# A linear-attention and MLP block on one core: projections in 64-row array tiles, key-value sums over blocks of both signs, and a token-major query side

## The chip, the core and the metric

The kernel runs on one core of a Trainium2 chip. The core has a matrix engine (PE, with its weight loads listed apart as PEld), a vector engine (DVE), a scalar engine (ACT), a general engine (POOL), a sequencer that here only issues DMAs (SP), and 16 DMA engines that all queues share. The metric is the device time of one execution in microseconds (us); lower is better. The kernel before takes 407.46 us, the median of three runs from 407.23 to 407.73.

## The reference

```
x: 1 x 2048 x 576 (bf16), 32 heads of 18;  LN = layer norm over the last axis
qkv   = LN(x) @ wqkv                          # 576 -> 3 x 576
pq,pk = q @ w_phi[h], k @ w_phi[h]            # per head, 18 -> 18
phi_q = [softmax(pq), softmax(-pq)]           # per head, 18 + 18 features
phi_k = [softmax(pk), softmax(-pk)]
kv    = sum_s phi_k[s]^T v[s];  z = sum_s phi_k[s]
o     = (phi_q @ kv) / (phi_q . z + 1e-6)
h     = x + o @ wo
h2    = h + gelu(LN(LN(h)) @ w1 + b1) @ w2 + b2   # 576 -> 4608 -> 576
```

The softmax over 18 features needs no maximum here: both kernels exponentiate and divide by the sum.

## The kernel before

The 2048 tokens are 16 token tiles of 128. `w_phi` is folded into the key and query weights first: the weight is transposed (`flip`, or five DMA transposes in `turn_wq`) and multiplied by a block-diagonal matrix of `w_phi` (`fold`, L271), so that one product gives all of pk or pq.

**Front: projections.** Each token tile is normalised on DVE (`normalise`, L208; some tiles on ACT, L236) and turned to feature-major form: the first four tiles on PE (`transpose_to`, L249), the others by DMA transposes (L243). The 576 features are cut into five chunks of 128 rows, the last one half empty. `project` (L307) multiplies one token tile by the value weights (`pv`) or the folded key weights (`pk`): five chunks by two column halves of 288, ten matmuls. ACT copies the values out (L318) and exponentiates the keys twice, with plus and minus sign (L329). DVE sums each head's features and inverts (`total`, L334), and POOL multiplies the keys by that (`weigh`, L342; L346). Queries are made the other way round (`ask`, L287): the folded weights are the stationary operand and 512 tokens the moving one, so the exponentials `eT` come out feature-major; 20 such units of five matmuls are spread between the key and value tiles. Query softmax sums are not taken at this point.

**Sums.** When all keys are weighed, `sums` (L505) makes ten accumulations over the 16 token tiles, one for each of five head groups and each of the two signs (`pkv`, L510; 160 matmuls), and DVE masks them to the block diagonal in `kvm` (L519, L524). `kvm` holds 20 columns a head: 18 values, the normaliser, and a column of ones that yields the query's softmax sum.

**Combine.** `combine` (L531) multiplies a token tile's `eT` by `kvm` in ten matmuls, in two units of heads (`pn`, L543). The two signs are weighted crosswise with each other's softmax sum: ACT copies those sums out (L551, L552), DVE multiplies (L555), POOL adds the signs (L561), DVE inverts and divides (L564, L565). The result `ob` is turned: on PE for tiles 0 to 3 (L586), by DMA for the rest (L582). `residual` (L591) multiplies by `wo` (ten matmuls `pa`, L598), adds to x and takes statistics on DVE; `rescale` writes the doubly normalised tile twice, side by side, into `ln2`; `turn2` (L619) turns it.

**MLP.** Eight strips of 256 tokens. `up` (L729) has 18 pairs of F-tiles; each pair is 9 chunks of 64 features by two matmuls that use rows 0-63 and rows 64-127 of the array (`ph`, L737), and ACT applies GELU (L761). `down` (L767) is 144 matmuls per strip (`po`, L782), then DVE adds (L786) and SP stores (L787). Between them `mlp` (L798) places the residual of the next strip's two tiles and the combines of the strip after that at given positions of `down` (`marks`).

**What sets the order.** PE and POOL follow the program text throughout. ACT, DVE and SP follow it through the front, up to `front.close()`; afterwards a scheduler orders them. A queue runs in order and stands still while its first instruction waits. All loads, stores and DMA transposes but three go through SP's queue. `w1` is loaded in two parts of six DMAs of 432 KB (`load_w1`, L417): the first at tile 11, the second, followed by twelve DMAs of `w2` (L720), once the keys' and values' memory is free, which is after the last of the sums.

```
nc.tensor.matmul(ph[half][:, cols], w1[..][rows, c, ..], x[rows, c, cols], ..)   # up, rows = 64 of 128
for m in range(0, NM // 2, 3): ... nc.sync.dma_start(w2[:, m0:m0+3, :], ..)      # L718-720, after load_w1(1)
work_ = [enter(a), enter(a+1), combine(b,0), leave(b), combine(b+1,0), leave(b+1)]; marks = [2,24,46,66,86,106]
```

Of the kernel before, what the change touches and what calls it, by code (L numbers as in the profile page):

```python
# [8 lines left out]
P = 128  # L9
# [11 lines left out]
NC = 5  # L21
# [7 lines left out]
NW = DH + 2  # L29
TB = 256  # L30
UNITS = [(0, 3), (3, 5)]
UH = 21
KC = 9
KH = 64


@with_exitstack
def kernel(
# [16 lines left out]
    NB = S // 512  # L55
    NS = S // TB
    TPS = TB // P

# [6 lines left out]
    e_pool = ctx.enter_context(tc.tile_pool(name="e_pool", bufs=4))  # L65
# [4 lines left out]
        tc.manual_schedule(engines={mybir.EngineType.PE, mybir.EngineType.Pool})  # L70
    )
    front = ctx.enter_context(ExitStack())
    front.enter_context(
        tc.manual_schedule(
            engines={
                mybir.EngineType.Activation, mybir.EngineType.DVE, mybir.EngineType.SP,
# [5 lines left out]
    wqp = persist.tile([P, NC, DP], BF16, name="wqp", tag="wqp")  # L82
    wo = persist.tile([P, NC, D], BF16, name="wo", tag="wo")
    kvm = persist.tile([P, NG, 2, 7 * NW], BF16, name="kvm", tag="kvm")
# [6 lines left out]
    ob = [persist.tile([P, DP], BF16, name=f"ob{i}", tag=f"ob{i}") for i in range(2)]  # L91

    psA = ctx.enter_context(ExitStack())
    two = psA.enter_context(tc.tile_pool(name="two", bufs=3, space=bass.MemoryType.PSUM))
    one = psA.enter_context(tc.tile_pool(name="one", bufs=2, space=bass.MemoryType.PSUM))
    w1_pool = ctx.enter_context(tc.tile_pool(name="w1_pool", bufs=1, side="left"))
    kctx = ctx.enter_context(ExitStack())
    kpool = kctx.enter_context(tc.tile_pool(name="kpool", bufs=1, side="left"))
    inner = ctx.enter_context(ExitStack())
    wpool = inner.enter_context(tc.tile_pool(name="wpool", bufs=1, side="right"))  # L100

    phik = [kpool.tile([P, 2, D], BF16, name=f"phik{t}", tag=f"phik{t}") for t in range(NT)]
    vals = kpool.tile([P, NT, NH, VW], BF16, name="vals", tag="vals")
    w1 = [w1_pool.tile([P, KC, FF // 4], BF16, name="w1_0", tag="w1_0")]
    wv = wpool.tile([P, NC, D], BF16, name="wv", tag="wv")
    wT = wpool.tile([P, NG, DP], BF16, name="wT", tag="wT")
    wkp = wpool.tile([P, NC, D], BF16, name="wkp", tag="wkp")
    bd = wpool.tile([P, NG, 7, DH], BF16, name="bd", tag="bd")
    wph = wpool.tile([P, NG, DH], BF16, name="wph", tag="wph")
    lnb = [wpool.tile([P, DP], BF16, name=f"lnb{i}", tag=f"lnb{i}") for i in range(6)]  # L110
# [8 lines left out]
    def scratch(n):  # L119
        e = e_pool.tile([P, NG, 2, 512], BF16, name="eT", tag="eT")  # L120
        flat = e[:, :, :, :].rearrange("p g s t -> p (g s t)")[:, 0 : NC * n]
        return flat.rearrange("p (c f) -> p c f", c=NC)

    wk = scratch(D)
    wq = scratch(DP)
    wphi_rows = A_w_phi.rearrange("h d f -> (h d) f")
    nc.scalar.dma_start(xh[:, 0:1, :], x_v[:, 0:1, :])
# [5 lines left out]
    nc.sync.dma_start(xh[:, 1:2, :], x_v[:, 1:2, :])  # L133
    load_rows(wv, A_wqkv[:, 2 * D : 3 * D])
    nc.sync.dma_start(xh[:, 2:4, :], x_v[:, 2:4, :])
    nc.sync.dma_start(xh[:, 4:8, :], x_v[:, 4:8, :])
    for c in range(NC):
        m = P if c < NC - 1 else 64
        src = A_wqkv[c * P : c * P + m, 0 : NG * 126]
        nc.sync.dma_start(  # L140
            wq[:m, c, :].rearrange("p (g f) -> p g f", g=NG)[:, :, 0:126],
            src.rearrange("p (g f) -> p g f", g=NG),
        )
    nc.sync.dma_start(xh[:, 8:16, :], x_v[:, 8:16, :])
# [15 lines left out]
    nc.gpsimd.memset(kvm[:, :, :, :], 0.0)  # L160
    for t_ in (wk, wv):
        nc.vector.memset(t_[64:P, 4, :], 0.0)
    nc.vector.memset(wq[64:P, 4, :], 0.0)
    nc.vector.memset(wq[:, :, :].rearrange("p c (g f) -> p (c g) f", f=P)[:, :, 126:P], 0.0)
    for i in range(6):
        nc.vector.memset(lnb[i][:, D:DP], 0.0)
    nc.vector.memset(wkp[64:P, 4, :], 0.0)
    spare = small.tile([P, 4], FP32, name="spare", tag="spare")
    nc.scalar.copy(spare[:, :], mhalf[:, :])
    nc.scalar.activation(  # L170
        vals[:, :, :, DH],
        ident[:, 0:NH].rearrange("p (o h) -> p o h", o=1).to_broadcast([P, NT, NH]),
        AF.Identity, bias=ones7[:, 0:1], scale=0.0,
    )
# [9 lines left out]

    def warm(n):
        pw = two.tile([P, P], BF16, name="pw", tag="two")
        for _ in range(n):
            nc.tensor.transpose(pw[:, :], ident[:, :], ident[:, :])

    def inverse(mv, n, bias, scale, eng=nc.vector):  # L190
        va = small.tile([P, 2], FP32, name="va", tag="va")
        eng.tensor_scalar(va[:, 0:n], mv[:, 0:n, 1], scale, bias, ALU.mult, ALU.add)  # L192
        rs = small.tile([P, 2], FP32, name="rs", tag="rs")
        nc.gpsimd.tensor_tensor(rs[:, 0:n], va[:, 0:n], mhalf[:, 0:n], ALU.pow)  # L194
        return rs

    def statistics(tiles, bias, scale, eng):
        n = len(tiles)
        mv = small.tile([P, 2, 2], FP32, name="mv", tag="mv")
        for i, t in enumerate(tiles):  # L200
            st = small.tile([P, 2, nc.vector.BN_STATS_DIM], FP32, name="st", tag="st")
            nc.vector.bn_stats(st[:, 0, :], xh[:, t, 0:HALF])
            nc.vector.bn_stats(st[:, 1, :], xh[:, t, HALF:D])
            nc.vector.bn_aggr(mv[:, i, :], st[:, :, :])
        return mv, inverse(mv, n, bias, scale, eng)
# [5 lines left out]

    lnT = [lnt_pool.tile([P, NC, 512], BF16, name="lnT", tag="lnT") for _ in range(NT // 4)]
    moments, shifts = {}, {}
# [8 lines left out]
    def measure(*tiles):  # L222
        mv, rs = statistics(tiles, EPS, 1.0, nc.vector if tiles[0] < 4 else nc.gpsimd)
        for i, t in enumerate(tiles):
            moments[t] = (mv, rs, i)
            if t >= 8 and t % 2:
                shifts[t] = shift(mv, rs, i)

    def turned(t):
        b, j = divmod(t, 4)  # L230
        return lnT[b][:, :, j * P : (j + 1) * P]

    def scale(t):
        if t >= 8 and t % 2:
            mv, rs, i = moments[t]
            nc.scalar.activation(  # L236
                lnb[t % 6][:, 0:D], xh[:, t, :], AF.Identity,
                bias=shifts[t][:, :], scale=rs[:, i : i + 1],
            )
        else:  # L240
            normalise(lnb[t % 6][:, 0:D], xh[:, t, :], *moments[t])
        if t >= 4:
            nc.sync.dma_start_transpose(turned(t), lnb[t % 6][:, :])  # L243

    def turn_wq(c0, c1):
        for c in range(c0, c1):
            nc.sync.dma_start_transpose(wT[:, :, c * P : (c + 1) * P], wq[:, c, :])

    def transpose_to(src, dst, copy=nc.scalar.copy):  # L249
        pT = one.tile([P, DP], BF16, name="pT", tag="one")  # L250
        for c in range(NC):
            nc.tensor.transpose(
                pT[:, c * P : (c + 1) * P], src[:, c * P : (c + 1) * P], ident[:, :]
            )
        copy(dst, pT[:, :].rearrange("p (c q) -> p c q", c=NC))  # L255
# [14 lines left out]

    def fold(wp, c, copy):  # L271
# [10 lines left out]
        copy(wp[:m, c, 0:D].rearrange("p (i f) -> p i f", i=2), pW[:m, :, 0:HALF])  # L282

    eT = {}
    banks = {"q": (one, "one")}

    def ask(b, g):  # L287
        if g == 0:
            eT[b] = e_pool.tile([P, NG, 2, 512], BF16, name="eT", tag="eT")
        pool, tag = banks["q"]  # L290
        pq = pool.tile([P, 512], FP32, name="pq", tag=tag)

        def part(c0, c1):
            for c in range(c0, c1):
                nc.tensor.matmul(  # L295
                    pq[:, :], wqp[:, c, g * 126 : g * 126 + P], lnT[b][:, c, :],
                    start=(c == 0), stop=(c == NC - 1),
                )

        part(0, 2)  # L300
        yield
        part(2, NC)
        yield
        nc.scalar.activation(eT[b][:, g, 0, :], pq[:, :], AF.Exp, scale=1.0)
        nc.scalar.activation(eT[b][:, g, 1, :], pq[:, :], AF.Exp, scale=-1.0)

    def project(dst, lhs, w):  # L307
        for c in range(NC):
            for i in range(2):
                nc.tensor.matmul(  # L310
                    dst[:, i, 0:HALF], lhs[:, c, :], w[:, c, i * HALF : (i + 1) * HALF],
                    start=(c == 0), stop=(c == NC - 1),
                )

    def value(t):
        pv = two.tile([P, 2, 512], FP32, name="pv", tag="two")
        project(pv, turned(t), wv)
        nc.scalar.copy(  # L318
            vals[:, t, :, 0:DH].rearrange("p (i h) d -> p i h d", i=2),
            pv[:, :, 0:HALF].rearrange("p i (h d) -> p i h d", d=DH),  # L320
        )

    rk = {}

    def key(t):
        pk = two.tile([P, 2, 512], FP32, name="pk", tag="two")
        project(pk, turned(t), wkp)
        for s in range(2):
            nc.scalar.activation(  # L329
                phik[t][:, s, :].rearrange("p (i f) -> p i f", i=2),  # L330
                pk[:, :, 0:HALF], AF.Exp, scale=1.0 - 2.0 * s,
            )
# [94 lines left out]
    def more():  # L427
        for _ in ask(*next(asked)):
            pass
# [427 lines left out]
```

## Time and profile before

| | value |
|---|---|
| median of three runs | 407.46 us (407.23 to 407.73) |
| span of the profiled execution | 405.5 us |
| span against that median | 2.0 us less |
| PE busy | 398.6 us, 98% |
| ACT, DVE, POOL busy | 196.8, 175.8, 107.0 us |
| up, first pair starts | 90.16 us |
| first matmul of the first down | 111.85 us |
| a strip of the MLP, steady state | 39.12 us (133.23 to 172.35) |

The profile was taken by the hardware on one execution; its own time is the span of 405.5 us, from the first to the last instruction, and the runs' median lies 2.0 us above it. A group's line reads: line of the program, engine, operation, tile written and tiles read, shapes, count; busy time of the group and mean time of one; idle time of the engine before it. Matmuls overlap, so the mean of one matmul is longer than its share of the engine: 324 matmuls of `up` take 17.79 us in the chain, 54.9 ns each, though one lasts 269 ns. Where this text gives a pace, it is such a quotient. The row "to landing" is the time from a DMA's issue to the arrival of its completion.

### The profile page before, as it was taken

The numbers are of one execution on the slowest core, as the hardware profiler recorded it, in microseconds if no ns is written. First come the engines' busy times: TensorE is split into PE (matmuls) and PEld (weight loads), VectorE is DVE, ScalarE is ACT, GpSimd is POOL, SyncE is SP. The second block draws the span as 40 slices with busy tenths as digits, with TensorE's granted clock in tenths as the row PEclk, the third lists the DMA queues.
The fourth block names the chain that finished last, engine by engine and source line by source line (L and its number), as shares of the span: only waits on it lengthen the run. The fifth ranks groups of instructions, "written<-read, shape, count | busy, mean of one in ns | idle before, by whom it ended". The sixth has DMA issues, their size and how long they took to land.

```text
span 405.5 us, 11185 instructions
## 1 busy us (share of the span) xinstructions
PE 398.6 (98%) x4882; PEld 324.2 (80%) x4882; DVE 175.8 (43%) x393; ACT 196.8 (49%) x468; POOL 107.0 (26%) x146
## 2 busy tenths in 40 slices
PE   7999999999999999999999999999999999999996
PEld 7786667758888888788888888888888888778875
DVE  5899975683466007601750274037204620510000
ACT  6888985388710680077008502840283048206800
POOL 5479994221214102310240023003200410111010
PEclk9999999999999999999999999999999999999999
DMA  8973586099712102200320032003200310220000
GB/s 250 229 109 49 129 169 131 17 224 325 229 32 61 32 2 53 49 23 2 60 51 15 2 70 52 2 3 73 49 3 14 78 33 3 19 55 18 2 16 15
DMA packets 52011, 27.83 MB, mean 69 GB/s; under 512 B 40506, under 2 KB 49274, under 8 KB 51834
## 3 DMA queue, kind: packets, MB, share of 16 engines
q1 hardware_dynamic: 51216, 26.95, 29.3%
q8 instruction: 38, 0.62, 0.6%
q10 hardware_dynamic: 746, 0.17, 0.2%
q14 instruction: 11, 0.09, 0.1%
HBM read 15.87 MB, written 2.36 MB: 45 GB/s over the span
## 4 chain that ended last, share of the span: by engine, by line
PE 90%; DMA 5%; DVE 1%; ACT 1%; SPq 1%; issue 1%; POOL 0%; DVEq 0%; ACTq 0%
PE ph L737 35%; PE po L782 35%; PE pa L598 5%; PE pv L310 3%; PE pq L295 3%; PE pk L310 3%; DMA w<-in_B_w_dram 2%; PE pn L543 2%; PE pkv L510 2%; DMA wT<-eT 1%; DMA eT<-in_A_wqkv_dram 1%; PE pW L276 1%; SPq L421 1%; DVE ln L208 0%; PE pT L586 0%
## 5 line engine op out<-in xcount | busy, mean ns | idle before, releaser
L761 ACT ACTIVATE h<-ph,b1col 128x256 bf16<-128x256 f32 x288 | 120.5, 470 | 75.0 <-PE ph L737 56.3
L782 PE MATMUL po<-w,h 128*128 128x288 bf16 x1152 | 148.7, 286 | 0.0
L737 PE MATMUL ph<-ln2T,w 64*128 64x256 bf16 (+1 forms) x2646 | 143.8, 267 | 0.0
L737 PEld LDWEIGHTS <-w 64*128 64x128 bf16 x2646 | 125.8, 94 | 17.1 <-issue 2.1
L782 PEld LDWEIGHTS <-h 128*128 128x128 bf16 x1152 | 110.9, 98 | 28.3 <-issue 1.5
L602 DVE TENSOR_TENSOR xh<-pa,xh 128x288 bf16<-128x288 f32 x32 | 14.4, 450 | 112.3 <-PE pa L598 112.3
L194 POOL TENSOR_TENSOR rs<-va,mhalf 128x1 f32<-128x1 f32 (+1 forms) x26 | 15.2, 583 | 155.3 <-DVE va L192 154.8
L551 ACT COPY sw<-pn 128x21 f32<-128x21 f32 (+1 forms) x32 | 5.6, 174 | 97.4 <-PE pn L543 97.3
L561 POOL TENSOR_TENSOR uu<-tt 128x399 f32<-128x399 f32 (+1 forms) x32 | 26.6, 832 | 69.7 <-DVE tt L555 67.8
L310 PEld LDWEIGHTS <-lnT 128*128 128x128 bf16 x320 | 30.7, 98 | 9.7 <-ACT lnT L255 0.3
L786 DVE TENSOR_TENSOR ot<-po,hb 128x288 bf16<-128x288 f32 x32 | 14.5, 453 | 53.9 <-PE po L782 53.9
L346 POOL TENSOR_TENSOR phik<-phik,rk 128x576 bf16<-128x576 bf16 x30 | 35.1, 1195 | 3.4 <-DVE rk L340 3.4
L772 POOL TENSOR_TENSOR hb<-xh,b2bc 128x576 f32<-128x576 bf16 x16 | 20.4, 1273 | 54.5 <-DVE ot L786 51.6
L555 DVE TENSOR_TENSOR tt<-pn,sw 128x798 f32<-128x798 f32 (+1 forms) x32 | 25.1, 785 | 6.9 <-ACT sw L552 6.8
L295 PE MATMUL pq<-lnT,wqp 128*128 128x512 bf16 x100 | 24.9, 379 | 0.1
L598 PE MATMUL pa<-wo,oT 128*128 128x288 bf16 x160 | 22.2, 286 | 0.1
L310 PE MATMUL pv<-wv,lnT 128*128 128x288 bf16 x160 | 22.2, 286 | 0.0
L310 PE MATMUL pk<-wkp,lnT 128*128 128x288 bf16 x160 | 22.1, 286 | 0.1
L336 DVE TENSOR_REDUCE sk<-phik 128x64 f32<-128x1152 bf16 x16 | 21.2, 1323 | 1.9 <-ACT phik L329 1.8
L565 DVE TENSOR_TENSOR ob<-uu,rec 128x378 bf16<-128x378 f32 (+1 forms) x32 | 21.0, 656 | 1.1
L329 ACT ACTIVATE phik<-pk 128x576 bf16<-128x576 f32 x32 | 19.2, 656 | 3.6 <-PE pk L310 3.6
L208 DVE TENSOR_SCALAR ln<-xh,mv,rs 128x576 bf16<-128x576 bf16 x31 | 16.3, 567 | 7.3 <-POOL rs L194 7.3
(82 smaller groups left out, 245.3 us busy)
## 6 DMA issues: line engine op xcount, KB each, us to landing
w<-in_B_w_dram SPq DMA_DIRECT2D x24, 432.0 KB, 9.1
out_dram<-ot SPq DMA_DIRECT2D x16, 144.0 KB, 1.8
xh<-in_A_x_dram SPq DMA_DIRECT2D x1, 1152.0 KB, 7.0
eT<-in_A_wqkv_dram SPq DMA_DIRECT2D x4, 157.5 KB, 6.3
eT<-in_A_wqkv_dram SPq DMA_DIRECT2D x1, 576.0 KB, 5.0
wv<-in_A_wqkv_dram SPq DMA_DIRECT2D x1, 576.0 KB, 6.5
xh<-in_A_x_dram SPq DMA_DIRECT2D x1, 576.0 KB, 7.6
wo<-in_A_wo_dram SPq DMA_DIRECT2D x1, 576.0 KB, 4.2
```

What stands on the lines that cost most here:

```text
L295: nc.tensor.matmul(pq[:, :], wqp[:, c, g * 126 : g * 126 + P], lnT[b][:, c, :], start=(c == 0), stop=(c == NC - 1),)
L310: nc.tensor.matmul(dst[:, i, 0:HALF], lhs[:, c, :], w[:, c, i * HALF : (i + 1) * HALF], start=(c == 0), stop=(c == NC - 1),)
L336: nc.vector.tensor_reduce(sk[:, :], phik[t][:, :, :].rearrange("p s (h f) -> p (s h) f", f=DH), AX.X, ALU.add)
L346: eng.tensor_tensor(fs, fs, rk[t][:, s, :].rearrange("p (h o) -> p h o", o=1).to_broadcast([P, NH, DH]), ALU.mult,)
L555: nc.vector.tensor_tensor(tt[:, :, 0:nh, :], pnv[:, :, :, 0:VW], sw[:, :, 0:nh].rearrange("p s (h o) -> p s h o", o=1).to_broadcast([P, 2, ...
L561: nc.gpsimd.tensor_tensor(uu[:, 0:nh, :], tt[:, 0, 0:nh, :], tt[:, 1, 0:nh, :], ALU.add)
L565: nc.vector.tensor_tensor(o[:, h0 * DH : (h0 + nh) * DH].rearrange("p (h d) -> p h d", d=DH), uu[:, 0:nh, 0:DH], rec[:, 0:nh].rearrange("p ...
L598: nc.tensor.matmul(pa[:, :], oTs[t][:, c, :], wo[:, c, cs], start=(c == 0), stop=(c == NC - 1),)
L737: nc.tensor.matmul(ph[half][:, cols], w1[p_ // 9][rows, c, p_ % 9 * P : (p_ % 9 + 1) * P], x[rows, c, cols], start=(c == 0), stop=(c == KC ...
L761: nc.scalar.activation(h1[m // 9][:, m % 9, :], ph[half][:, :], AF.Gelu_apprx_tanh, bias=b1col[:, m : m + 1], scale=1.0,)
L772: nc.gpsimd.tensor_tensor(hb[:, :], xh[:, t, :], b2bc[:, :], ALU.add)
L782: nc.tensor.matmul(po[:, :], h1[m // 9][:, m % 9, i_ * P : (i_ + 1) * P], w2[:, m, cs], start=(n == 0), stop=(n == NM - 1),)
```

## The change

- **Projections.** Features are cut into nine chunks of 64. The normalised tiles of two token tiles are interleaved by chunk, so that one turned tile holds chunk c of the first token tile in rows 0-63 and of the second in rows 64-127. `project` then runs two matmuls of 64 rows for each chunk, one for each token tile, into two PSUM banks: 18 matmuls of 288 columns for two token tiles and one column half. The weights must stand in both row halves: `wv` is loaded twice, `wkp` and `wqp` are copied across by three DMAs each (`double`), `wo` is loaded twice, 32 rows at a time, in four DMAs. The first five of nine chunk pairs in `CROSSED` use the rows as `fold` left them. `residual` uses the same form for two token tiles.
- **Features.** Keys and queries are both made token-major by `features`; the two signs of a head stand side by side, 36 columns a head, 1152 in all. Queries are normalised too (`norm_q`: DVE sum and reciprocal, two POOL products) and turned by two DMA transposes of 128 x 1152 a pair (`turn_q`).
- **Sums.** `sums(p)` accumulates nine windows of 128 feature columns for each token tile into two PSUM banks, as soon as a pair's keys are weighed: 144 matmuls of 76 or 95 columns. `table` masks all of it after the last.
- **Combine.** One product: ten matmuls a tile give numerator and denominator; `divide` is a reciprocal and two products on DVE, reading PSUM. ACT and POOL have no part in it. The tile `pn` has one buffer, as before in the MLP.
- **Turning and order.** Tiles go in pairs. On PE are turned: the first two pairs of x, the first pair of `ob`, the first pair of `ln2`; all others by DMA, the second pair of `ob` among them. All five engines follow the program text throughout. In each strip the residual of the next pair stands between `up` and `down`, the combines at positions 20 and 50 of `down`, and `norm_q` at 64 and 100. SP's order is: first loads, `double(wkp)`, `wq`, second half of x, turns of pairs 2 and 3, `turn_wq`, turn of pair 4, `double(wqp)`, `wo`, biases, turns of pairs 5 to 7, first part of `w1`, `turn_q(0)`, `turn_q(1)`, second part of `w1`, `w2`, `turn_q(2)`, `turn(1)`, `turn2` of tiles 2 and 3, and so on.
- **Memory.** The front's weights `wk`, `wq`, `wT`, `bd`, `wph` borrow the space of the first part of `w1`; `lnb`, `wkp`, `ln2`, `oT` and `ln2T` share one region.

```diff
+    def load_values(i):
+        src = A_wqkv[:, 2 * D + i * HALF : 2 * D + (i + 1) * HALF]
+        for half in range(2):
+            nc.sync.dma_start(
+                wv[half * KH : (half + 1) * KH, :, i * HALF : (i + 1) * HALF],
+                src.rearrange("(c k) f -> k c f", k=KH),
+            )
...
+    def scale(p):
+        mv, rs, nb = moments[p]
+        normalise(lnb[p % 3][:, :, 0, :], chunks(2 * p), mv, rs, 0)
+        shifted(lnb[p % 3][:, :, 1, :], chunks(2 * p + 1), rs, nb, 1)
+        if p >= 2:
+            nc.sync.dma_start_transpose(
+                turned(p), lnb[p % 3][:, :, :, :].rearrange("p c a k -> p (c a k)")
+            )
...
+    def double(wp):
+        nc.sync.dma_start(wp[KH:P, 8, :], wp[0:KH, 8, :])
+        nc.sync.dma_start(wp[0:KH, 1:8:2, :], wp[KH:P, 0:8:2, :])
+        nc.sync.dma_start(wp[KH:P, 1:8:2, :], wp[0:KH, 0:8:2, :])
+
+    def project(dst, lhs, w, i, order):
+        for n, pick in enumerate(order):
+            for a in range(2):
+                rows = slice(a * KH, (a + 1) * KH)
+                c = pick[a]
+                slot = pick[0] if order is CROSSED else c
+                nc.tensor.matmul(
+                    dst[:, a, 0:HALF], lhs[rows, c, :], w[rows, slot, i * HALF : (i + 1) * HALF],
+                    start=(n == 0), stop=(n == KC - 1),
+                )
...
+    def normal(dst, i, engines):
+        part = dst[:, :, i * D : (i + 1) * D].rearrange("p a (h f) -> p a h f", f=DH)
+        nc.vector.tensor_reduce(sk[:, :, :], part, AX.X, ALU.add)
+        nc.vector.reciprocal(rk[:, :, :], sk[:, :, :])
+        for a, eng in enumerate(engines):
+            eng.tensor_tensor(...)
...
+    def turn_q(p):
+        for a in range(2):
+            nc.sync.dma_start_transpose(phiT[p][:, a, :, :], phiq[p][:, a, :])
+
+    def sums(p):
+        for a in range(2):
+            t = 2 * p + a
+            for w in range(KC):
+                nc.tensor.matmul(acc_kv[...], phik[p][:, a, w * P : (w + 1) * P], vals[...], ...)
...
+    wo_v = A_wo.rearrange("(h c e) f -> e h c f", c=KC, e=2)
+    for half in range(2):
+        for e in range(2):
+            r0 = half * KH + e * 32
+            nc.sync.dma_start(wo[r0 : r0 + 32, :, :], wo_v[e])
...
+    key(4, 0)
+    value(4, 0)
+    norm_k(3, 0)
+    scale(5)
+    key(4, 1)
+    value(4, 1)
+    norm_k(3, 1)
+    sums(0)
+    sums(1)
+    key(5, 0)
+    query(0, 0)
+    norm_k(4, 0)
+    value(5, 0)
+    measure(6)
+    key(5, 1)
+    query(0, 1)
+    norm_k(4, 1)
+    value(5, 1)
+    scale(6)
...
+    turn(0, True)
+    norm_q(1, 0)
+    query(6, 1)
+    first = residual(0, double_bank)
+    for _ in first:
+        pass
+    norm_q(1, 1)
     rescale(0, True)
+    query(7, 0)
+    query(7, 1)
+    turn_q(1)
+    turn2(0, True)
     rescale(1)
     load_w1(1)
     for m in range(0, NM // 2, 3):
         for m0 in (m, m + NM // 2):
             nc.sync.dma_start(w2[:, m0 : m0 + 3, :], w2v[:, m0 : m0 + 3, :])
...
+        if s_ == 0:
+            rises = {
+                5: lambda: combine(2 * a),
+                10: lambda: (combine(2 * a + 1), turn(a)),
+                2: lambda: norm_q(b, 0),
+                8: lambda: (norm_q(b, 1), turn_q(b)),
+            }
...
+        h1 = next(rise)
+        if a < NS:
+            for _ in residual(a, two_banks):
+                pass
+            for t in (2 * a, 2 * a + 1):
+                rescale(t)
+                turn2(t)
+        if b < NS:
+            falls[20] = lambda: combine(2 * b)
+            falls[50] = lambda: (combine(2 * b + 1), turn(b))
+        if c < NS:
+            falls[64] = lambda: norm_q(c, 0)
+            falls[100] = lambda: (norm_q(c, 1), turn_q(c))
+        down(s_, h1, falls)
```

801 lines of the change are left out of this document (343 added, 458 removed).

## The prediction

> **What bounds the kernel now.** I read the page's busy shares first, then the chain that ended last, then the groups, and then, because the change moves many loads and turns, SP's own timeline and the DMA rates by window.
>
> ```profile
> PE 398.6 (98%) x4882; PEld 324.2 (80%) x4882; DVE 175.8 (43%) x393; ACT 196.8 (49%) x468; POOL 107.0 (26%) x146
> PE 90%; DMA 5%; DVE 1%; ACT 1%; SPq 1%; issue 1%; POOL 0%; DVEq 0%; ACTq 0%
> ```
>
> PE is the bound: busy 98%, and 90% of the chain. So matmul time taken away is worth its full length, but only as long as nothing makes PE wait, and before almost nothing does. The groups give the prices:
>
> ```profile
> L737 PE MATMUL ph<-ln2T,w 64*128 64x256 bf16 (+1 forms) x2646 | 143.8, 267 | 0.0
> L295 PE MATMUL pq<-lnT,wqp 128*128 128x512 bf16 x100 | 24.9, 379 | 0.1
> L310 PE MATMUL pv<-wv,lnT 128*128 128x288 bf16 x160 | 22.2, 286 | 0.0
> L346 POOL TENSOR_TENSOR phik<-phik,rk 128x576 bf16<-128x576 bf16 x30 | 35.1, 1195 | 3.4 <-DVE rk L340 3.4
> L336 DVE TENSOR_REDUCE sk<-phik 128x64 f32<-128x1152 bf16 x16 | 21.2, 1323 | 1.9 <-ACT phik L329 1.8
> ```
>
> The reader should see in the first that 64-row matmuls run two at a time: 324 of them take 17.79 us in the chain, 54.9 ns each for 256 columns. The last two are the price of normalising, which the change now pays for queries too. SP's timeline and the waits on it show the cover that is thin:
>
> ```profile
> 78.72 3.88 SPq L421 DMA_DIRECT2D w<-in_B_w_dram  x6
> 83.44 18.64 SPq L720 DMA_DIRECT2D w<-in_B_w_dram  x12
> ```
>
> These 18 DMAs (7.96 MB) are issued from 78.7 us, the moment the sums end; the last issue is at 101.0 and lands some 8.7 us later, at 109.7. The first `down` starts at 111.85. The loads take 31 us and are hidden with 2 us to spare. Two windows show their rates (last columns: clock, DMA share, GB/s), `w1` into 64 partitions, then `w2` into 128:
>
> ```profile
> 60.00:64.00 4.00, 4.00 (x27) 2.52 (x26) 3.86 (x4) 3.42 (x7) 3.56 (x3) 1.00 1.04 214
> 100.00:104.00 4.00, 4.00 (x73) 3.37 (x71) 1.30 (x4) 3.08 (x10) 0.49 (x1) 1.00 1.09 355
> ```
>
> And the chain has one turn that was issued behind a load:
>
> ```profile
> 14.08 6.03 DMA wT<-eT
> ```
>
> A DMA transpose issued at 14.08, behind the 1152 KB of x issued at 12.39, reaches its consumer after 6.0 us, when x also lands; the turns of `ob`, with nothing in front, land after 2.6. Turns go through the queue behind the loads. That decides this forecast.
>
> **The change part by part: matmul time.** A half-width 64-row product for two token tiles is 18 matmuls of 288 columns: 18 x 54.9 x 288/256 = 1.11 us, so 2.22 for two tiles where the chain shows 2 x 1.23 = 2.46. Values and keys save 8 x 0.24 x 2 = 3.8 us, the output projection 1.9. Queries: 20 units of 1.08 become 8 x 2.22 = 17.8, saving 3.8. Sums: the chain has 5.93 + 1.90 + 1.12 = 8.95 us; 144 matmuls with 760 columns a token tile, at the chain's pace for a 440-column `pn` group (about 0.2 us), take 0.36 x 16 = 5.7, saving 3.3. Combine: 0.57 a tile becomes 0.36, saving 3.3. Turns on PE: 1.3. Together 17.4 us. Each visit of a 128-row product among 64-row ones costs 0.1 (six `pn` take 0.48 inside `up`, 0.37 inside `down`); the front has about 14, half of them inside waits below.
>
> **Work off PE.** Gone are ACT's and POOL's part of the combine (L551, L552, L561: 32 us) and DVE's L555 and L565 (46 us). Added: query sums on DVE, 16 x (1.32 + 0.55) = 30 us, POOL products 32 x 1.16 = 37 us, `divide` 16 x (0.35 + 2 x 0.45) = 20 us (reciprocal between the rows for 21 and 64 columns, products as L602, also 288 from PSUM), 16 turns of 1152 columns, double the loads of `wv` and `wo`, six copies. None of it is long in total; what counts is what stands behind what. I walked the five queues and the DMA queue in the changed order with these durations (value copy 0.64, exponential 0.60, scale on ACT 0.87, turn 1.2 to issue and 3.2 to land). PE waits:
>
> - Pair 2's turn. `double(wkp)` is issued at 17 (its last fold copy sits on ACT behind the scale of pair 1), `wq` and 1152 KB of x behind it: 3.1 + 2.7 + 3.6 us of transfer, then the turn lands at 29.5. PE has used up pairs 0 and 1 at 26.2: 3.3 us.
> - Pair 5's turn. It stands on SP behind `double(wqp)` (waits for the query fold, 42), four `wo` loads and the biases: 3.1 + 6.2 + 0.5 + 1.7 lands it at 56.3; PE stands at `key(5, 0)` from 48.5: 7.8 us. The query matmuls that need no new turn stand behind it.
> - Pair 6's turn needs ACT's scale, which is behind the copy of `value(5, 1)`: 0.64 + 0.87 + 3.2, less one query unit: 4.1 us; pair 7 likewise 0.9.
> - First combine. `norm_q(0)` is on POOL behind the last keys (four products of 1.16 after the last reciprocal), then two turns: 2.4 + 1.3 us.
> - First residual. `norm_q(1, 1)` stands ahead of the row shift on POOL and of the rescale on DVE: from the residual's end at 102.6, statistics 2.6, sum and reciprocal 1.9, two products 2.3, shift 0.4, ACT 0.9; the two query units cover only 2.2 of it: 6.8 us before the first `ln2` is turned.
>
> That puts the end of `norm_q(1, 1)` at 110.3 and the start of `up` at 114.6, where it was at 90.16.
>
> Prices no row shows: an SBUF-to-SBUF copy (between 64 partitions at 355 and at half of 214 GB/s; I take 214, the nearest, 3.1 us each set) and a load into 32 partitions (`wo`, 1.33 MB: 3.7 us at 355, 12.3 at half of 214; taken at 214, 6.2). Their ends move the 110.3 to 107 and 116.
>
> **The loads.** The second part of `w1` and `w2` now stand on SP behind `turn_q(1)`: issue from 110.3 + 2.4 = 112.7, and with the same 31 us `w2` has landed at 143.6. `turn(1)`, which `residual(1)` needs, is issued after `w2` and two more turns, some 1.7 us of transfer each: 147.9. `up` runs from 114.6 to 137.9 (17.8 matmul, 0.7 turn, 0.7 combine, 3.6 waiting for `w1`), so PE stands 10 us. Here cover that was there before (turn on PE, loads 31 us ahead of need) is gone.
>
> **The rest.** From 147.9: seven residuals of 2.22, 15.5; `down` 8 x 144 x 122.5 ns = 141.1; seven `up`, 124.5; 12 combines, 4.3; tail after the last matmul 3.1 as now: 288.5. In each of six strips DVE has, after the end of `up`, the residual's adds, statistics and four rescales (some 0.5 us each, done at 8.4 us) before `divide` of the first combine, done at 9.9; PE reaches the second combine, which needs the one `pn` buffer, at 8.8: 1.1 us x 6 = 6.6 (between 0, if the divide is early, and twice that, as L565's mean of 0.66 against its best 0.36 allows). Span: 147.9 + 288.5 + 6.6 = 443.0; the profiled span lies 2.0 under the runs' median, so **445**.
>
> **A rule against it.**
>
> ```profile
> L188 PE MATMUL pw<-ident 128*128 128x128 bf16 x40 | 4.4, 313 | 1.4 <-POOL mhalf L149 1.4
> 91.34 0.68 PE pT L640 x9
> ```
>
> The first 40 transposes take 111 ns each, nine later ones in the chain 76: a cold start of PE cost 1.4 us, though the granted clock reads 1.00. The Trainium skill (TensorE: Matmul & The Clock Gate, Part 1) says PE falls back to half clock after about 3.4 us of idleness and needs as long of work to recover; by it each long wait costs up to an estimated 1.7 us more. The trace of before has no such wait to test it on. By the row, three waits over 3.4 us on the path (7.8, 4.1, 10) add 3 x 1.4 = 4 us: 449, part of the third rival.
>
> **The rivals.**
> 1. Turns do not queue behind the loads. For it: only one row shows them queued, and the other turns land in 2.6 to 4.2. Then pair 2 waits 0.5, pair 5 3.0; `norm_q(1, 1)` ends at 104.8, `turn(1)` lands at 134.0, before `w2` at 137: 134 + 295 + 2 = 431; 424 without the `pn` waits.
> 2. PE's work alone decides: each turn and each load is in time, as all are now. The place is SP's queue at the second part of `w1`: price 17.4 us, 390. It decides only if `norm_q(1, 1)` ends by about 80 us, as the sums do now (78.7); with all front waits at nothing the walk still gives 84, with loads until 117 and 405 to 411. For it speaks a front that is 98% dense now with 17 turns in it; against it that each wait above follows from the written order.
> 3. Narrow loads or cold restarts. `wo` at half rate: `norm_q(1, 1)` ends at 116.4, 451; with the cold starts 455, and the `pn` wait doubled 460.
> 4. 64-row products of two token tiles do not run side by side: 36 matmuls of 288 columns at 120 ns each, 53 us more, 498. L737 has the same form and does run so; nearly excluded.
>
> **How the numbers follow.** Chances: forecast 0.50 (its own range 436 to 452), rival 1 0.25, rival 2 0.07, rival 3 0.15, rival 4 and the unnamed 0.03. The range, 418 to 460, runs from rival 1 without `pn` waits and a little less front wait to rival 3's end. A difference within 0.2% (0.8 us) is what the runs can't tell from none. Faster holds most of rival 2 (0.06), same 0.02, slower 0.92.
>
> **What would show it.** Right: PE slices well under 9 before `up`; waits of PE's weight loads on DMA `lnT` at `key(5, 0)` and `value(2, 0)`; `up` starting near 115; SP's `w2` issues ending near 134; a wait of 6 to 12 us for `oT` between the first `up` and `down`; later strips near 39 us, with short waits of `pn` on DVE L580. Wrong: PE 95% busy, `w2` landed by 115, or turns that land in 3 us while loads are open. The forecast fails most likely in how turns and loads share the queue.

## The result, and the profile after

The changed kernel takes 447.05 us (median of 4 runs, 445.2 to 448.35), the kernel before 407.4 beside it: a ratio of 1.097, 95% interval 1.0941 to 1.0995. The change is 9.7% slower; the forecast was 445. The profiled execution has a span of 445.1 us and a time of 446.8. Three executions further below ran at a lower granted clock than the others of their kernel (the turn on PE 529.3 us at 0.745, five lots of dummies 701.0 at 0.561, the third rewrite 417.8 at 0.970) and are left out of every number; the first two are the profiled ones, so no stage of these two kernels is read.

First the page of the changed kernel: busy time of the engines, then in 40 slices of 11.1 us PE's busy tenths and the tenths of the clock granted to it, then the chain that ended last.

```profile
PE 395.4 (89%) x5425; PEld 322.8 (73%) x5425; DVE 168.5 (38%) x350; ACT 184.3 (41%) x394; POOL 110.9 (25%) x124
...
PE   6849566997596599999999999999999999999997
...
PEclk8978968999699599999999999999999999999999
...
PE 48%; issue 14%; DVE 12%; DMA 8%; SPq 8%; POOL 5%; ACT 4%; POOLq 0%; DVEq 0%
```

PE was 98% busy and is 89% busy, 50 us idle instead of 7. All of the holes lie in the first 14 slices, the first 156 us; behind them PE is as dense as before. And PE, which made up 90% of the chain, makes up 48%: DVE, POOL, DMA and SP's queue have entered it.

Next PE's timeline, at the longer waits (start, duration, line, operation, shapes, and in brackets the idle time before and what ended it), from the pair-2 turn to the first residual that stands between an `up` and a `down`:

```profile
31.46 2.34 PE L337 MATMUL pv<-wv,lnT 64*128 64x288 bf16 x18 [5.86 <-DMA lnT<-shared]
...
59.95 2.34 PE L337 MATMUL pk<-shared,lnT 64*128 64x288 bf16 x18 [8.27 <-DMA lnT<-shared]
...
72.90 2.10 PE L337 MATMUL pk<-shared,lnT 64*128 64x288 bf16 x18 [3.61 <-DMA lnT<-shared]
...
99.66 0.54 PE L598 MATMUL pn<-kvm,phiT 128*128 128x76 bf16 x10 [0.50 <-DMA phiT<-phiq]
100.99 0.54 PE L598 MATMUL pn<-kvm,phiT 128*128 128x76 bf16 x10 [0.79 <-DMA phiT<-phiq]
...
115.30 1.14 PE L285 MATMUL pT<-ident,shared 128*128 128x128 bf16 x9 [6.16 <-ACT shared L243]
117.92 1.15 PE L721 MATMUL ph<-shared,w 64*128 64x128 bf16 x18 [1.49 <-ACT shared L287]
131.81 0.50 PE L721 MATMUL ph<-shared,w 64*128 64x256 bf16 x5 [0.93 <-DMA w<-in_B_w_dram]
150.07 4.50 PE L629 MATMUL pa<-wo,shared 64*128 64x288 bf16 x36 [9.27 <-DMA shared<-ob]
```

The brackets add up to 37.2 us (with 0.35 for pair 7, not shown). `up` starts at 117.92, where it started at 90.16: 27.8 later. From there to the end it is 327.2, where it was 315.3: 11.9 more, and the last of these waits alone is 9.3. SP's timeline says why the last one is so long:

```profile
115.82 3.90 SPq L516 DMA_DIRECT2D w<-in_B_w_dram  x6
119.83 19.28 SPq L700 DMA_DIRECT2D w<-in_B_w_dram  x12
139.21 7.39 SPq L397 DMA_TRANSPOSE phiT<-phiq  x2
146.70 1.32 SPq L613 DMA_TRANSPOSE shared<-ob  x1
...
169.72 2.72 SPq L397 DMA_TRANSPOSE phiT<-phiq  x2
```

The rows of `turn(1)` were ready at 134. Its DMA is issued at 146.70, behind 18 loads that went out from 115.82 and behind `turn_q(2)`. The two transposes of `turn_q(2)` take 7.4 us to go out, where the next two, on an empty queue, take 2.7.

### The profile page after: what moved, and what is told of

It reads as the page before. It is cut to its first block, busy times and chain, and to the rows that moved or that the text cites. A ratio compares the mean times of both kernels' runs of the same rounds, so it can differ in the third digit from the quotient of the medians.

```text
span 445.1 us, 12094 instructions
## 1 busy us (share of the span) xinstructions
PE 395.4 (89%) x5425; PEld 322.8 (73%) x5425; DVE 168.5 (38%) x350; ACT 184.3 (41%) x394; POOL 110.9 (25%) x124
## 4 chain that ended last, share of the span: by engine, by line
PE 48%; issue 14%; DVE 12%; DMA 8%; SPq 8%; POOL 5%; ACT 4%; POOLq 0%; DVEq 0%
PE ph L721 20%; PE po L766 20%; DMA lnT<-shared 5%; SPq L700 4%; POOL phiq L380 3%; PE pk L337 3%; PE pa L629 2%; DVE shared L231 2%; DVE sk L376 2%; DMA xh<-in_A_x_dram 2%; SPq L397 2%; DVE st L636 2%; PE pv L337 2%; DVE xh L635 1%; POOL rs L227 1%
## 5 line engine op out<-in xcount | busy, mean ns | idle before, releaser
L721 PE MATMUL ph<-shared,w 64*128 64x256 bf16 (+1 forms) x2646 | 145.1, 269 | 2.5 <-ACT shared L287 1.5
L337 PEld LDWEIGHTS <-lnT 64*128 64x128 bf16 x864 | 44.0, 100 | 35.4 <-DMA lnT<-shared 20.0
L380 POOL TENSOR_TENSOR phiq<-phiq,rk 128x576 bf16<-128x576 bf16 x32 | 36.5, 1162 | 52.9 <-DVE rk L378 52.9
L337 PE MATMUL pk<-shared,lnT 64*128 64x288 bf16 x288 | 22.9, 310 | 12.9 <-DMA lnT<-shared 12.2
L629 PE MATMUL pa<-wo,shared 64*128 64x288 bf16 x288 | 21.1, 303 | 9.3 <-DMA shared<-ob 9.3
L337 PE MATMUL pv<-wv,lnT 64*128 64x288 bf16 x288 | 21.3, 294 | 7.6 <-DMA lnT<-shared 5.9
L231 DVE TENSOR_SCALAR shared<-xh,mv,rs 128x576 bf16<-128x576 bf16 x39 | 19.8, 555 | 9.2 <-POOL rs L227 9.2
L355 ACT ACTIVATE phiq<-pk 128x576 bf16<-128x576 f32 x32 | 18.9, 648 | 8.6 <-PE pk L337 6.2
L337 PE MATMUL pk<-wqp,lnT 64*128 64x288 bf16 x288 | 21.4, 296 | 0.0
L376 DVE TENSOR_REDUCE sk<-phiq 128x64 f32<-128x1152 bf16 x16 | 21.4, 1339 | 0.0
```

Source lines behind the costliest of these rows:

```text
L231: nc.vector.tensor_scalar(dst, src, mv[:, i, 0:1], rs[:, i : i + 1], ALU.subtract, ALU.mult)
L337: nc.tensor.matmul(dst[:, a, 0:HALF], lhs[rows, c, :], w[rows, slot, i * HALF : (i + 1) * HALF], start=(n == 0), stop=(n == KC - 1),)
L355: nc.scalar.activation(rows[:, :, i * HH : (i + 1) * HH, s, :], pk[:, :, 0:HALF].rearrange("p a (h f) -> p a h f", f=DH), AF.Exp, scale=1. ...
L376: nc.vector.tensor_reduce(sk[:, :, :], part, AX.X, ALU.add)
L380: eng.tensor_tensor(part[:, a, :, :], part[:, a, :, :], rk[:, a, :].rearrange("p (h o) -> p h o", o=1).to_broadcast([P, NH, DH]), ALU.mult,)
L629: nc.tensor.matmul(pa[a], oT[p % 2][rows, c, :], wo[rows, c, cs], start=(c == 0), stop=(c == KC - 1),)
```

## Experiments

Theory A (queues): the time is set by what stands behind what on SP, ACT and POOL; work that is moved out of the way gives the time back. Theory B (work): the added normalising, turning and loading has to be paid wherever it stands. Theory C (clock): part of a wait's price is the halved clock behind it. Each kernel differs from the changed one by the edit shown; each median stands beside 407.2 to 407.8 for the kernel before. No kernel leaves work out; four add dummy transposes. How far two timelines can be compared, the front shows: up to the first `pn` the changed kernel and four of the others (the rescale's, the one with `w1` early, those with 100 and 155 dummies) have the same work in the same order, and yet it starts anywhere from 97.88 to 101.68.

**The turn behind `w2`, made on PE.**

```diff
-                10: lambda: (combine(2 * a + 1), turn(a)),
+                10: lambda: combine(2 * a + 1),
+                14: lambda: turn(a, True),
```

> One edit to the changed kernel: the turn of the second attention strip (turn(1), needed by residual(1)) is made on TensorE with nine transposes at pair 14 of the first up, instead of by a DMA issued behind the loads of w2. Theory A (queues: the time is set by what stands behind what on SP and in the DMA queue): the 9.3 us wait for oT before residual(1) goes, 0.7 us of PE is added, and the next late thing is w2 itself, whose last part lands near 147, some 4 to 5 us after residual(1) now ends, so only part is won: 436 to 439. Theory B (work: the added normalising, turning and loading has to be paid wherever it stands): the wait moves to the next place in full, 446 to 448.

Measured: 439.3 (437.7 to 440.9), ratio 1.0785 (1.075 to 1.0821), 8 us less than the changed kernel. That is A's direction, 0.3 beyond its 436 to 439; B would have kept 446 to 448. Whether the end of `w2` is what binds next, as A says, is not shown.

**The rescale ahead of `norm_q(1, 1)`.**

```diff
-    norm_q(1, 1)
     rescale(0, True)
+    norm_q(1, 1)
```

> One edit to the changed kernel: the first rescale is issued ahead of norm_q(1, 1), so the row shift and the scaled rows no longer stand behind two query products on POOL. If every wait of PE costs what it shows (the sum of the prediction taken as additive), the first up starts 5 us earlier and the time is 442. Theory A (queues): up does start about 4 to 5 us earlier, but norm_q(1, 1) then ends 1 to 3 us later, and with it the issue of w1's second part and of w2, and of the turn behind them, so residual(1) starts at 150 to 152 as before and the wait ahead of it grows from 9.3 to about 15: 446 to 449. Theory B (work): 446 to 448, with up starting at the same time.

Measured: 450.2, ratio 1.1061 (1.1036 to 1.1086): 3 us slower, with a wait of PE shortened, and 1 us beyond A's range. The timelines of PE and SP:

```profile
113.94 0.68 PE L285 MATMUL pT<-ident,shared 128*128 128x128 bf16 x9 [2.78 <-ACT shared L243]
...
155.27 4.50 PE L629 MATMUL pa<-wo,shared 64*128 64x288 bf16 x36 [8.21 <-DMA shared<-ob]
```

```profile
120.16 3.88 SPq L516 DMA_DIRECT2D w<-in_B_w_dram  x6
...
151.92 1.32 SPq L613 DMA_TRANSPOSE shared<-ob  x1
```

The wait ahead of the turn fell from 6.16 to 2.78, but the loads start 4.3 us later and the last turn 5.2 (151.92 for 146.70). Of that, 2.0 us are older than the edit: the first `pn` starts at 101.68 for 99.66. Then `up` itself stood 6.3 us for `w1`, where it stood 0.93. Waits don't add: this one was cover for the loads. A had the direction and, less those 2.0, its 1 to 3 us of delay; the wait of about 15 us that it foresaw ahead of `residual(1)` came as 6.3 and 8.21.

**The second part of `w1` early.**

```diff
     kctx.close()
+    w1b_pool = ctx.enter_context(tc.tile_pool(name="w1b_pool", bufs=1, side="left", ...))
+    w1.append(w1b_pool.tile([P, KC, FF // 4], BF16, name="w1_1", tag="w1_1"))
+    load_w1(1)
...
-    load_w1(1)
```

> One edit to the changed kernel: the second part of w1 gets its own pool and is issued right after the tile memory of the keys is free (near 98 us), before the turns of the second pair, instead of after them near 116. w2 stays where it was in the order. Theory A (queues): the six w1 loads are done by about 108, w2's twelve loads take about 15 us less to finish, the turn of the second strip lands before up ends, and residual(1) starts at about 139 to 141 instead of 150; with the clock not dropping there as well, 433 to 437. Theory B (work): the same bytes have to go through the same DMA queue, the turn stays behind them, 446 to 448.

Measured: 433.5, ratio 1.064 (1.0619 to 1.0661); 13.6 us less, with the same bytes and the same products. The timelines of SP and PE:

```profile
97.25 3.88 SPq L516 DMA_DIRECT2D w<-in_B_w_dram  x6
111.13 2.75 SPq L397 DMA_TRANSPOSE phiT<-phiq  x2
113.99 11.42 SPq L703 DMA_DIRECT2D w<-in_B_w_dram  x12
129.59 3.57 SPq L397 DMA_TRANSPOSE phiT<-phiq  x2
133.26 1.32 SPq L618 DMA_TRANSPOSE shared<-ob  x1
```

```profile
138.53 2.37 PE L634 MATMUL pa<-wo,shared 64*128 64x288 bf16 x36
```

`turn(1)` goes out at 133.26, and the first residual starts at 138.53 without a wait and at full pace (2.37 instead of 4.50). It starts 11.5 us earlier, of which 1.8 were there at the first `pn`, ahead of the edit. B falls for this stage.

**`wo` behind the turns of pairs 5 to 7.**

```diff
-    (the four loads of wo and the two of the biases, ahead of measure(5))
...
     scale(7)
+    (the same six loads)
```

> One edit to the changed kernel: the four loads of wo and the two of the biases are issued after scale(7), behind the turns of pairs 5 to 7, instead of ahead of them. Theory A (queues): pair 5's turn, whose rows are ready near 49.8, is issued then and lands near 53 to 54; the wait before key(5, 0) falls from 8.3 to 1 to 2 us and the clock does not drop behind it (2 us more); pair 6's wait of 3.6 stays, since ACT's order makes it. Of 7 + 2 us all reaches the end, since nothing else in the front was waiting on the loads: 437 to 440. Theory B (work): the loads have to be paid later, before residual(0) or w1: 445 to 448.

Measured: 445.95, ratio 1.0951 (1.0932 to 1.0969): 1 us, not 8. The wait at `key(5, 0)` did fall from 8.27 to 2.09. It came back 40 us on, in PE's and SP's timelines:

```profile
96.40 0.82 PE L598 MATMUL pn<-kvm,phiT 128*128 128x76 bf16 x10 [4.60 <-DMA phiT<-phiq]
```

```profile
72.98 2.63 SPq L535 DMA_DIRECT2D wo<-in_A_wo_dram  x4
75.65 0.61 SPq L536 DMA_DIRECT2D b1nat<-in_B_b_dram  x1
76.32 0.37 SPq L537 DMA_DIRECT2D b2bc<-in_B_b_dram  x1
76.73 5.57 SPq L507 DMA_DIRECT2D w<-in_B_w_dram  x6
89.07 6.27 SPq L397 DMA_TRANSPOSE phiT<-phiq  x2
```

`wo` and the first part of `w1` now go out together, ahead of the first pair's `turn_q`, whose transposes take 6.3 us to go out instead of 2.7. The expectation ("nothing else in the front was waiting on the loads") was wrong; the mechanism was A's own, one turn further on. `residual(1)` starts at 148.29, 1.8 us earlier, and that is the gain.

**`norm_q(1)` with the first pair's.**

```diff
     turn_q(0)
+    norm_q(1, 0)
...
     combine(1, two)
+    norm_q(1, 1)
+    turn_q(1)
...
     turn(0, True)
-    norm_q(1, 0)
...
-    norm_q(1, 1)
     rescale(0, True)
...
-    turn_q(1)
     turn2(0, True)
```

> One edit to the changed kernel: norm_q(1, 0), norm_q(1, 1) and turn_q(1), whose queries exist from about 76 us, are issued right behind the first pair's (near 97 to 104 us) instead of between and behind the two steps of the first residual. Theory A (queues): the first rescale no longer stands behind them on POOL (up starts 3 to 4 us earlier), and the loads of w1's second part and w2 start near 109 instead of 116, so that the turn of the second strip lands near 140 and residual(1) starts there: 434 to 438. Theory B (work): DVE and POOL have as much to do as before ahead of up, and the combines now wait for it: 445 to 449.

Measured: 441.1, ratio 1.0828 (1.0781 to 1.0876). The loads start at 108.20 instead of 115.82, `turn(1)` goes out at 138.98 instead of 146.70, `residual(1)` starts at 143.24 instead of 150.07: the chain moves by what its head moves. It missed A's 434 to 438 by 3 us: the turn still lands 4.5 us after PE needs it, and the first residual still takes 4.50.

**Dummy transposes in the waits.** First five lots, then one lot of 100 or 155 ahead of `residual(1)` alone.

```diff
+            if s_ == 0:
...
+                for _ in range(155):
+                    nc.tensor.transpose(pw2[:, :], ident[:, :], ident[:, :])
             for _ in residual(a, two_banks):
```

> The changed kernel with dummy transposes of the identity added on TensorE in five of its waits (before value(2, 0), key(5, 0), key(6, 0), the first turn2 and residual(1): 55, 85, 35, 55 and 90 of them, results unused, each lot shorter than its wait). Nothing else is moved. Clock theory: the half clock that the records show after each of these waits (a half-width product takes 2.34 instead of 1.10 us, the first residual 4.5 instead of 2.2) goes, and about 8 us with it: 438 to 442. If the slow products after a wait only fill time that another wait would take, 446 to 448. If the dummies themselves are on the path because a lot outlasts its wait, up to 450.

> The changed kernel with 100 dummy transposes of the identity (results unused) between the first up and residual(1) alone, where PE stands 9.3 us for a turn. Clock theory: residual(1) takes 2.2 to 2.5 us instead of 4.5, and the time is 444 to 445. Otherwise residual(1) stays at 4.5 and the time at 446 to 448.

> As with dummy transposes in one wait, but 155 of them, which fill the wait before residual(1) to within about 0.7 us of its end instead of 3.4. Clock theory (the clock falls some 3 to 4 us after the last product, and rises only after some 5 us of work): residual(1) takes 2.2 to 2.5 us instead of 4.5, the products behind it are at full pace too, and the time is 444 to 445. Otherwise 446 to 448.

Measured: 444.7, ratio 1.0926 (1.0903 to 1.0948), at a granted clock of 0.976; 446.7, ratio 1.0972 (1.0911 to 1.1034); 447.1, ratio 1.0979 (1.0957 to 1.1). The first residual with 100 and with 155 dummies:

```profile
151.63 4.50 PE L629 MATMUL pa<-wo,shared 64*128 64x288 bf16 x36 [3.38 <-DMA shared<-ob]
```

```profile
152.31 2.38 PE L629 MATMUL pa<-wo,shared 64*128 64x288 bf16 x36 [1.50 <-DMA shared<-ob]
```

Idle for 3.38 us, PE works at half pace; idle for 1.50, at full pace. So the pace behind this wait is halved by the clock, as C says. The time didn't follow. With 155 dummies the residual saved 2.1 us but began 2.2 us later than without: the turn went out 0.8 us later, 0.6 of which were there at the first `pn`, and took 4.8 us to land, where it took 3.3 without dummies and with 100. Why it landed later, when only PE does more, isn't settled. Five filled waits gave 2.4 us by the medians, with intervals that overlap, where C had 8.

**Orders changed together.** All the work is kept; the second and third rewrite share the products of `norm_q(0)` between POOL and DVE, and the third adds 25 dummies.

> The changed kernel with the work as it is and five orders changed: wq and the last 1152 KB of x behind the turns of pairs 2 and 3; measure and scale of pairs 5 to 7 two to three steps earlier; wo behind them; norm_q(1) and turn_q(1) with the first pair's; the second part of w1 issued when the keys are done. Theory A (queues): nearly all of the 37 us of waits named in the trace go, with 6 to 8 us of low clock behind them; PE's own work, the tail and 5 to 8 us of small new waits are left: 404 to 412. If PE's saved 17.4 us were real and nothing else stood in the way it would be 390 to 400. Theory B (work: ACT and DVE can't prepare a pair in PE's time): 420 to 435, with waits of PE on ACT and DVE in the front.

> The changed kernel's work in one rewritten order. On SP: x tokens 8 to 11 in the gap ahead of pair 2's turn, then wq, pair 3's turn, pair 4's, the turns of wq, the last of x, the turns of pairs 5 to 7, wo, w1. The fold of the query weights stands behind pair 4, queries begin one pair later, both norm_q(1) stand ahead of the table, the halves of the first residual have a query unit between them, turn(1) is issued before the turns of the third queries, and the second combine of a strip stands 10 products of down later. Theory A (queues): against the version with five orders changed (426.9) the 16 us around the fold's wait for wq's turns go to about 3, and 1 to 2 us each at the first turn2, at residual(1) and in the six strips' waits for pn: 404 to 411. Theory B: PE's work in the front with its real small gaps, or ACT and DVE, need more than PE's time: 414 to 424, with the waits spread over DVE and ACT and none of them long.

> The rewritten order once more, with what its trace showed late put right: the last 576 KB of x are issued ahead of the turns of wq, scale(5) to scale(7) stand one to two steps later on ACT (where they held up the exponentials that PE waited for), and the products of norm_q(0) are shared between POOL and DVE. Against 421.1 (417.6 in the profiled execution), theory A (queues) takes off the 2.1, 6.4 and 1.5 us waits around the fold of the query weights and some 4 us of half clock behind them, and about 1 us at the first combines: 406 to 411. Theory B (ACT, DVE and POOL need more than PE's time in the front): the waits come back at other places, 414 to 421.

> The second rewrite with its last 20 us before up put in another order: both norm_q(1) behind the table instead of ahead of it (they held it up for 4.2 us), the bias turned earlier, query(5, 1) ahead of the first combine, the first residual in one piece, its rescale behind the last query on ACT, and 25 dummy transposes (results unused) in the 2 us that PE then waits for the first turn2. Theory A (queues and clock): up starts 2 to 4 us earlier than at 98.5, and the clock, which fell to 0.50 at 84 and again at 98 us, stays up, another 2 to 3 us: 405 to 409, so level with the kernel before or 0.5% faster. Theory B: the chain of turn, divide, residual, statistics and rescale is bound by DVE and the turns whatever the order, 410 to 413.

Measured: 426.9, ratio 1.0486 (1.0458 to 1.0513); 421.1, 1.0357 (1.0328 to 1.0387); 412.2, 1.012 (1.0099 to 1.0142); 414.2, 1.016 (1.0139 to 1.0182). All four missed A's range, the second rewrite by 1 us; the first two lie in B's (420 to 435, 414 to 424), the other two in neither. In the first, `wq` stood so far behind the turns of pairs 2 and 3 that PE waited 7.9 us for its turns and 4.0 more at the fold behind a scale on ACT. In the second, the last of x stood behind the turns of `wq`: a scale waited on ACT, behind it the exponentials that PE needed, 2.1 and 6.4 us. PE's lines, two of the first and two of the second:

```profile
45.44 0.71 PE L315 MATMUL pW<-w 128*64 128x126 bf16 x6 [7.91 <-DMA w<-w]
...
52.15 1.17 PE L315 MATMUL pW<-w 128*128 128x126 bf16 x12 [3.96 <-ACT wqp L321]
```

```profile
42.45 1.28 PE L337 MATMUL pv<-wv,lnT 64*128 64x288 bf16 x18 [2.09 <-ACT phik L355]
...
51.34 1.69 PE L315 MATMUL pW<-w 128*128 128x126 bf16 x18 [6.42 <-ACT phik L355]
```

With that mended, the second rewrite has left of all waits of PE these over 1.3 us:

```profile
1.41 3.78 PE L221 MATMUL pw<-ident 128*128 128x128 bf16 x40 [1.41 <-POOL mhalf L171]
6.58 0.73 PE L301 MATMUL pX<-ident,w 128*128 128x128 bf16 x10 [1.39 <-DMA w<-in_A_wqkv_dram]
...
44.38 2.13 PE L315 MATMUL pW<-w 128*64 128x126 bf16 x30 [1.46 <-DMA w<-w]
...
82.57 1.50 PE L605 MATMUL pn<-kvm,phiT 128*128 128x76 bf16 x20 [4.19 <-DVE kvm L421]
...
96.36 1.05 PE L285 MATMUL pT<-ident,shared 128*128 128x128 bf16 x9 [1.71 <-ACT shared L243]
```

It stands 1.2% above the kernel before, so 34.9 of the 39.7 us went with the order, and not with the amount of work. `up` starts at 98.1 (before: 90.2), and from there to the end it takes 312.1 (before: 315.3). The third rewrite took `norm_q(1)` from ahead of the table; PE then waited 3.51 for the first query turn, and `up` started at 98.01:

```profile
82.71 0.54 PE L611 MATMUL pn<-kvm,phiT 128*128 128x76 bf16 x10 [3.51 <-DMA phiT<-phiq]
```

By what released PE there, DVE, POOL and the turns bind the last 20 us ahead of `up`, as B had it for this stretch. No kernel took work away from them, so this is read from waits and not tested. The expectation of 405 to 409 fell. The profiled execution took 410.2 at a granted clock of 0.991, five others 413.2 to 415.0 at 0.978 to 0.979; what the clock did in those no profile shows. No version was faster than the kernel before.

## Why the prediction came out right

Its end was 445 and its path was the measured one, but several terms were off and cancelled; that it came within 2 us is in part luck.

- **Pair 2's turn:** 3.3 us, measured 5.86. The loads in front of it were to be through at 26.4. By windows of 1 us the DMA engines still move 283 GB/s from 27 to 28 and 78 from 28 to 29, and the turn, issued at 22.90, is there at 31.4 instead of 29.5; PE had run out 0.6 us earlier than worked out.
- **Pair 5's turn:** 7.8, measured 8.27, standing where it was to stand, from 51.7 instead of 48.5. From the 42 that the prediction starts at, the terms that it names add up to 53.5 and not to its 56.3; the three copies of `double(wqp)` went out from 44.41, which is most of what it does not name. Pair 6: 4.1, measured 3.61, and 3.6 by the terms it names. Pair 7: 0.9, measured 0.35. First combines: 2.4 and 1.3, measured 0.50 and 0.79.
- **First rescale:** 6.8, measured 6.16 and 1.49. Late were POOL's two products of `norm_q(1, 1)`, 2.28 us ending at 114.1, ahead of the shift (0.26 us) that ACT waited for: the step as worked out, 3.8 us later than its 110.3 (109.4 by the terms it names). The unknown price of `wo` was not the cause; its four loads landed in 7.7 us (median), the turn behind them at 59.9, and the wait there was 8.27 for 7.8.
- **`up`** at 114.6: measured 117.92. It was to take 22.8 us by its terms (which end it at 137.4, not at the 137.9 that is given), 3.6 of them waiting for `w1`; it took 22.9 with 0.93 of waiting. The halved clock behind the 6.16 filled the gap: its first 18 products took 1.15, where the kernel before has 0.68.
- **Loads:** issue from 112.7, measured 115.82. `turn(1)` to land at 147.9: measured 150.0, the wait 9.27 where 10 was worked out. Taking `w1`'s second part out of this chain gave 13.6 us back, and making the turn on PE 8, so the step is shown, not only argued.
- **The rest:** 295.1 from there to the end, measured 295.0, and this is the cancelling. The six `pn` waits were to cost 6.6 together; PE stood at five of them, 0.38 to 0.44 each, 2.0 together: 4.6 us too much. The halved clock behind the long wait was in no term of the sum: the first residual takes 4.50, the later ones 2.37, and the first 20 products of `down` behind it 2.74 instead of 2.46. The other 2 us are small: later residuals and downs each take 0.1 to 0.3 more than their terms. A strip takes 39.09 where it took 39.12, because the `pn` wait and a little more eat what the products save:

```profile
230.00 2.37 PE L629 MATMUL pa<-wo,shared 64*128 64x288 bf16 x36
...
239.42 0.53 PE L598 MATMUL pn<-kvm,phiT 128*128 128x76 bf16 x10 [0.44 <-DVE ob L580]
```

With the second combine ten products later that wait is gone, and a strip takes 38.47 (141.18 to 179.65 in the second rewrite): 0.65 less than before, and the prediction's terms, 0.24 for the residual and 2 x 0.21 for the combines, sum to 0.66.
- **PE's work:** 17.4 us saved. PE's busy time fell from 398.6 to 390.1 in the second rewrite, at a clock of 0.979, and to 388.0 in the third, at 0.991 and with 1.6 us of dummies in it: 8.5 to 12 us, less than the term, though products at half pace are still in both.

Of the rivals, the first (turns don't queue behind loads) falls with SP's rows above. The second (PE's work alone, 390) falls too: the waits that it takes to be absent were there, and the best of four orders came to 412. With PE's busy time down by 8.5 to 12 us, 395 to 399 is the estimate without waits, not 390. The third had a cold restart as its mechanism. That exists, and by the rows it is larger than the 1.4 us a wait that the prediction took. What it costs in time isn't shown: 447.05 lies between the forecast and this rival's first step of 449, and dummies in the waits gave 0 to 2.4 us. The fourth (no side by side) falls with 18 products in 1.10 us; by its own rows (2.1 us more for two tiles, 32 times) its price was 67, not 53.

## What to carry to other kernels

A turn by DMA shares its queue with every load issued before it: to move a turn from PE to DMA, list what is issued in the 30 us ahead of it, and put big loads behind the turns that someone waits for, or far ahead of them. A wait that is removed shows the next one in the same queue; what the edit gives is the later start of the last joint of that chain, not the sum of the brackets. When a change moves work onto engines that had slack, ask for the stretch with the least slack: here 20 us in which DVE and POOL were both needed to feed PE, and none of the four orders hid it.

## What was not expected of the hardware

**The clock.** The prediction's trace had no long wait; these runs have many. The product behind a wait ran at full pace after waits of 1.50, 1.75 and 2.78 us, and at about half after 3.38, 5.86, 8.27 and 9.27. The length of the wait alone doesn't decide it. After 3.51 the first `pn` took 0.54 and the second 0.82. After 3.61 the product took 2.10 in the changed kernel and 1.28 with `wo` late, where only the one behind it was slow:

```profile
66.29 1.28 PE L337 MATMUL pk<-shared,lnT 64*128 64x288 bf16 x18 [3.61 <-DMA lnT<-shared]
67.40 2.27 PE L337 MATMUL pk<-wqp,lnT 64*128 64x288 bf16 x18
```

Behind the 2.78 the clock fell at the next wait (18 products of `up` in 1.15, for 0.68), and in the second rewrite it fell after a wait of only 1.71 (nine transposes in 1.05, for 0.68). Windows of 1 us around the wait of 9.27 (behind the length: PE, PE loads, DVE, ACT, POOL, the granted clock, then DMA share and GB/s):

```profile
144.00:145.00 1.00, 0.00 (x0) 0.00 (x0) 0.00 (x0) 0.00 (x0) 0.00 (x0) 0.94 1.51 313
145.00:146.00 1.00, 0.00 (x0) 0.00 (x0) 0.00 (x0) 0.00 (x0) 0.00 (x0) 0.50 1.27 116
...
154.00:155.00 1.00, 1.00 (x9) 0.36 (x6) 0.64 (x2) 0.00 (x0) 0.00 (x0) 0.50 0.00 0
155.00:156.00 1.00, 1.00 (x9) 0.80 (x8) 0.93 (x4) 0.00 (x0) 0.00 (x0) 0.94 0.00 0
```

PE's last product ended at 140.8; the clock fell at 144.9, 4.1 us later, and came back at 155.1, after 5.0 us of work. With 100 dummies, by the same windows, it fell 2.1 us after the last one and came back after 5.6 us; at the wait of 1.71 it fell 1.9 us after the last product (0.75 from 96 to 97, then 0.50). The Trainium skill (TensorE: Matmul & The Clock Gate, Part 1) states one idle window of about 3.4 us for the fall and as long of sustained work for the return, with windows that run freely. The fall 4.1 us after the last product agrees with it. Falls after 2.1 and 1.9 us leave no room for a window of that length without work. In the second rewrite short waits stood ahead of the fall (PE 70% busy from 93 to 94, 66% from 94 to 95), so less than full idleness seems to have been enough there; no run tests it. The return took longer than one such window.

**The issue of a DMA transpose.** It holds SP: 1.3 us on an empty queue, 4.7 us (the first of `turn_q(2)`, from 139.21) right behind the `w2` loads. What stands behind it on SP then starts that much later.
